# Soft-MoE attention kernel: the first pair's k exchange on ScalarE, the second pair's loads and splits ahead of the bias batches, another order of the attention steps

## The chip, the core and the metric

The kernel runs on one NeuronCore of a Trainium2 chip. Five engines work side by side, each on its own instruction queue, in order: TensorE (PE in the rows; PEld is its weight load), VectorE (DVE), ScalarE (ACT), GpSimd (POOL) and SyncE (SP), which here does nothing but issue DMA transfers. They wait for one another by semaphores. The metric is the device time of one execution in microseconds, as the median of several runs.

## The reference

Attention with a position bias made by a small network, then a soft mixture of experts, then a routed mixture of experts. Cut to what matters here:

```python
# q, k, v: (4, 8, 576, 64)
scores = scale * np.matmul(q, k.transpose(0, 1, 3, 2))
psi_rel = np.log1p(np.abs(rel)); psi_i = np.log1p(np.maximum(pos, 1.0))
h = np.maximum((psi_rel / psi_i)[..., None] @ w1 + b1, 0.0)   # hidden 32
bias = h @ w2                                                 # (576, 576, 8)
attn = softmax(scores + bias.transpose(2, 0, 1)[None])
x = (attn @ v).transpose(0, 2, 1, 3).reshape(2304, 512)
# soft MoE: logits = x @ phi; slots; 8 experts; combine; then a routed MoE
```

## The kernel before

**Stages.** The program has four stages. First come constants. Then **36 bias batches** (`bias_batch`, lines 193 to 215) compute the bias of all heads once and write it to a DRAM tile, `scratch`. Then **16 attention pairs** (a pair is two heads of one of four batches, `ops_of`, line 310) run in a software pipeline. Last come the two expert stages, for which 33 MB of weights are loaded; most of these loads are held until the last transpose DMA of attention (`issue_after(last_dma[0].ins)`, line 818).

**A bias batch** makes four tiles `hid` of 128x576 (line 204 on DVE for three of them, and in 27 of the 36 batches line 206 on ACT for the fourth), multiplies each with two matmuls (line 208) into one of two PSUM buffers `sc`, evicts that on ACT into `ev` (line 211) and writes `ev` to `scratch` by a DMA on SP (line 213). `hid` has 12 buffers, `ev` has six.

**A pair's inputs.** `LK` and `LQ` (lines 333 and 338) load k and q into `tk` and `tq`, one buffer each. On POOL, `KHI`, `KLO`, `QHI`, `QLO` (lines 374 and 376, called the splits below) split them into a high and a low part, `sk` and `sq`, one buffer each. PE transposes those (lines 407 and 432), ACT evicts them (lines 414, 437, 438) into `k0` and the `qT` tiles. `SW` (line 421, on POOL) writes `k1`, which is `k0` with its two halves of 64 partitions exchanged. So the next pair's `LK` waits until `KLO` has read `tk`, the next pair's `LQ` until `QLO` has read `tq`, and the next pair's `KHI` until PE has transposed all of `sk`.

**A pair's work.** For nine tiles: score matmuls from `k0` and `k1` (`QK..p`, line 449), bias added and row minimum on DVE (`QK..e`, line 466), exponential on ACT (`EX..`, line 473). Three double tiles are split into two f16 halves (`HI` on POOL, line 484; `LO` on DVE, line 488), transposed by a DMA (`TD`, line 493, tile `eT`) and multiplied with v (`AV`, lines 574 and 578). The rest goes through PE transposes and line 586. Line 395 splits v on POOL.

**What sets the order.** Each step has a place in the table `SCHED` (or `LAST`, for the last four pairs), in units of a planner's clock, with `II = 14100` units from one pair to the next. All steps are sorted by pair times `II` plus place. Those placed before the first score matmul are emitted ahead of the bias batches (lines 784 to 789), the others behind them, in a region in which every engine keeps exactly the emitted order (`manual_schedule`, line 806). Outside such a region the framework's scheduler orders each queue by its own estimate and may pull the first steps of the region forward among the bias batches.

Of the kernel before, what the change touches and what calls it, by code (L numbers as in the profile page):

```python
# [35 lines left out]
SCHED = {"LK": 5369, "LQ": 0, "LV": 10563, "BA": 23667, "BM": 30989, "TD0": 37335, "TD1": 43011, "TD2": 36576,  # L36
         "KHI": 6999, "KLO": 10045, "QHI": 5298, "QLO": 11325, "VA": 19235, "VH": 21228, "VLO": 27550, "KG0p": 11467,
# [11 lines left out]
LAST = {"LK": [-3065, 3082, 4354, 5430], "LQ": [-995, -2408, -2168, -2345], "LV": [10067, 14234, 12275, 20450],  # L49
         "BA": [18431, 35072, 34832, 22492], "TD0": [39915, 48050, 36190, 24610], "TD1": [49170, 48930, 36590, 25210],  # L50
         "TD2": [37091, 35430, 35150, 24410], "KHI": [3849, 7705, 6112, 5590], "KLO": [7665, 7785, 8536, 5670],
         "QHI": [7168, 4291, 6072, 6590], "QLO": [11035, 10644, 11635, 7150], "VA": [19244, 19466, 20650, 21450],
# [53 lines left out]
def soft_moe_attention_kernel(ctx, tc, q, k, v, w1, b1, w2, phi, mw1, mw2,  # L106
# [203 lines left out]
    def ops_of(n):  # L310
# [106 lines left out]
        @part  # L417
        def SW():
            k0, k1 = kk()
            for i in range(2):  # L420
                pool.tensor_scalar(out=k1[64 * i:64 * i + 64], in0=k0[64 - 64 * i:128 - 64 * i],  # L421
                                   scalar1=1.0, scalar2=1.0, op0=ALU.mult, op1=ALU.mult)
# [363 lines left out]
    for t_, n, x in todo:  # L786
        if t_ < first:
            OPS[n][x]()
# [583 lines left out]
```

## Time and profile before

| what | value |
|---|---|
| median of three runs | 495.49 us (495.05 to 497.6) |
| profiled execution: its time | 498.0 us |
| profiled execution: its span, first to last instruction | 496.2 us |
| mean granted TensorE clock | 0.952 |
| busy in the span: PE, DVE, ACT, POOL | 84%, 70%, 60%, 53% |

By time in the span: constants up to 7.1 us; bias batches to 77.2 us, with the first score result on DVE at 78.7 us; attention to about 350 us; the expert stages to the end. How to read the rows below: a busy row is one instruction or several merged; an idle time names what ended it; a wait names the waiting engine and line, an arrow, and what it waited for.

### The profile page before, as it was taken

To read this page: it belongs to the slowest core of one execution; us is meant where nothing else is said; L and a number is where in the kernel's file an instruction comes from. 1 tells how busy PE (TensorE), PEld (TensorE's weight loads), DVE (VectorE), ACT (ScalarE), POOL (GpSimd) and SP (SyncE) were. 2 spreads that over 40 slices of the span, in tenths; PEclk is the share of its full clock that TensorE was granted. 3 is DMA by queue.
4 is the path that set the end of the run, shared out by engine and by line. 5 is a ranking of instruction groups with operands and counts; after the bars stand their busy time and mean duration, and the time that the engine had idled before them with its cause. 6 is when DMAs were issued, how large, how long until landed. Compare 5 with 4: busy or idle time off the path is not lost.

```text
span 496.2 us, 11535 instructions
## 1 busy us (share of the span) xinstructions
PE 414.4 (84%) x4291; PEld 301.4 (61%) x4291; DVE 346.7 (70%) x824; ACT 298.5 (60%) x631; POOL 262.9 (53%) x245
## 2 busy tenths in 40 slices
PE   4870799797998999889899899897788787779993
PEld 2430356697987899769788799785345311255462
DVE  6990596888887899878889888897547400047564
ACT  3970796788887889779779799783322100027510
POOL 4496001999898799798978788861300000000000
PEclk9995799899999999999999999999899799959998
DMA  6713975799999999999998999799999999572066
GB/s 164 250 49 82 360 274 194 162 193 223 223 215 220 211 212 228 178 228 208 225 215 205 221 178 207 159 205 189 399 387 408 387 387 387 202 264 77 26 198 188
DMA packets 154076, 111.49 MB, mean 225 GB/s; under 512 B 120256, under 2 KB 126912, under 8 KB 154016
## 3 DMA queue, kind: packets, MB, share of 16 engines
q1 hardware_dynamic: 152112, 107.47, 85.8%
q10 hardware_dynamic: 1824, 2.97, 1.8%
q8 instruction: 36, 0.59, 0.5%
q0 software_dynamic: 80, 0.26, 0.2%
q14 instruction: 24, 0.20, 0.1%
HBM read 66.97 MB, written 15.34 MB: 166 GB/s over the span
## 4 chain that ended last, share of the span: by engine, by line
PE 41%; DMA 28%; DVE 10%; issue 8%; ACT 6%; POOL 4%; SPq 1%; ACTq 0%; DVEq 0%; POOLq 0%
DMA eT<-ehl 17%; PE sc L449 9%; DMA x<-in_moe_w_dram 4%; PE av L578 4%; PE sc L208 4%; POOL k L421 3%; PE av L586 3%; PE pt L407 3%; DVE e L466 3%; DMA bias<-in_moe_w_dram 2%; ACT ev L211 2%; PE ph L892 2%; DMA tn<-in_v_dram 2%; PE av L574 2%; DMA w1e<-in_moe_w_dram 1%
## 5 line engine op out<-in xcount | busy, mean ns | idle before, releaser
L466 DVE CUSTOM_DVE_ANT_0 e<-sc,bias 128x576 f32<-128x576 f32 x128 | 93.9, 749 | 25.0 <-PE sc L449 18.8
L449 PE MATMUL sc<-k,qT 128*128 128x288 f32 x512 | 98.6, 318 | 8.6 <-DVE st L466 5.5
L473 ACT ACTIVATE e<-e,st 128x576 f32<-128x576 f32 x128 | 97.3, 779 | 3.5 <-DVE st L466 3.0
L484 POOL TENSOR_SCALAR ehl<-e 128x1152 f16<-128x1152 f32 x48 | 66.1, 1383 | 53.1 <-ACT e L473 49.9
L488 DVE SCALAR_TENSOR_TENSOR ehl<-e,ehl 128x1152 f16<-128x1152 f32 x48 | 81.5, 1699 | 2.1 <-POOL ehl L484 2.1
L449 PEld LDWEIGHTS sc<-k,qT 128*128 128x128 f32 x512 | 73.1, 191 | 15.1 <-DVE st L466 8.4
L421 POOL TENSOR_SCALAR k<-k 64x1152 fp32r<-64x1152 f32 x32 | 75.0, 2343 | 12.6 <-ACT k L437 11.1
L208 PE MATMUL sc<-hid,w2b 128*32 128x288 f32 x576 | 50.0, 440 | 22.4 <-ACT ev L211 19.3
L204 DVE TENSOR_SCALAR hid<-ll,nib 128x576 f32<-128x576 f32 x117 | 53.6, 537 | 16.4 <-PE sc L208 16.4
L208 PEld LDWEIGHTS sc<-hid,w2b 128*32 128x32 f32 x576 | 24.2, 115 | 46.0 <-ACT ev L211 31.9
L578 PE MATMUL av<-v,eT 128*128 128x65 f16 x1152 | 50.2, 193 | 0.0
L578 PEld LDWEIGHTS <-eT 128*128 128x128 f16 x1152 | 42.8, 97 | 1.3 <-issue 0.8
L211 ACT ACTIVATE ev<-sc,offs,ipi 128x576 f32<-128x576 f32 x36 | 30.0, 834 | 21.8 <-DMA scratch<-ev 16.9
L1099 POOL TENSOR_SCALAR Lt<-rk 128x128 f16<-128x128 f32 x1 | 0.3, 298 | 74.3 <-PE pbig L973 74.3
L574 PE MATMUL av<-v,eT 128*128 128x130 f16 x144 | 16.3, 221 | 15.9 <-DMA eT<-ehl 15.9
L586 PE MATMUL av<-eq,tv 128*64 128x192 f32 x320 | 29.5, 331 | 0.0
L979 DVE COPY part<-pbig 128x256 f32<-128x256 f32 x1 | 0.4, 425 | 38.6 <-ACT part L978 38.6
L414 ACT ACTIVATE qT<-pt 128x512 fp32r<-128x512 f32 x32 | 19.1, 602 | 9.8 <-PE pt L407 9.5
L586 PEld LDWEIGHTS av<-eq,tv 128*64 128x64 f32 x320 | 21.6, 137 | 4.9 <-issue 2.4
L574 PEld LDWEIGHTS <-eT 128*128 128x128 f16 x144 | 9.8, 98 | 23.9 <-DMA eT<-ehl 22.1
L978 ACT COPY part<-pbig 128x256 f32<-128x256 f32 x1 | 0.4, 372 | 39.6 <-PE pbig L973 39.6
L395 POOL TENSOR_TENSOR v<-tv,v 128x650 f16<-128x650 f32 x16 | 24.0, 1502 | 0.0
(334 smaller groups left out, 887.2 us busy)
## 6 DMA issues: line engine op xcount, KB each, us to landing
x<-in_moe_w_dram SPq DMA_DIRECT2D x30, 512.0 KB, 10.7
scratch<-ev SPq DMA_DIRECT2D x36, 288.0 KB, 4.5
bias<-scratch SPq DMA_DIRECT2D x16, 576.0 KB, 4.8
tn<-in_v_dram SPq DMA_DIRECT2D x32, 224.0 KB, 4.3
bias<-in_moe_w_dram SPq DMA_DIRECT2D x13, 512.0 KB, 10.2
k<-in_moe_w_dram SPq DMA_DIRECT2D x12, 512.0 KB, 10.2
tq<-in_q_dram SPq DMA_DIRECT2D x16, 288.0 KB, 5.8
tk<-in_k_dram SPq DMA_DIRECT2D x16, 288.0 KB, 4.0
```

Of the source, the lines that this page charges most:

```text
L204: vec.tensor_scalar(out=hid, in0=src, scalar1=nib[:, gi:gi + 1], scalar2=None, op0=ALU.max)
L208: pe.matmul(pb[c * 32:(c + 1) * 32, hh, 0:288], lhsT=w2b, rhs=hid[:, hh * 288:(hh + 1) * 288], start=True, stop=True)
L211: act.activation(ev, pb[:, :, 0:288].rearrange("p a (l u) -> p u a l", u=NU), AF.Identity, bias=offs[not on_act], scale=ipi[:, bt:bt + 1])
L421: pool.tensor_scalar(out=k1[64 * i:64 * i + 64], in0=k0[64 - 64 * i:128 - 64 * i], scalar1=1.0, scalar2=1.0, op0=ALU.mult, op1=ALU.mult)
L449: pe.matmul(sc[:, hh, 0:288], lhsT=l_, rhs=kf[i][:, o:o + 288], start=(i == 0), stop=(i == 1))
L466: vec.tensor_tensor_reduce(out=z["e", t][:, o].rearrange("p (a j) -> p a j", a=2), in0=z.pop(("sc", t, j))[:, :, 0:288], in1=bias_t[hp, t] ...
L473: act.activation(ee, ee, AF.Exp, bias=z["m", t][:, j:j + 1], scale=-1.0, **kw)
L484: pool.tensor_scalar(out=eh[:, 0], in0=z["e", t], scalar1=ES, scalar2=1.0, op0=ALU.mult, op1=ALU.mult)
L488: vec.scalar_tensor_tensor(out=eh[:, 1], in0=z.pop(("e", t)), scalar=ES, in1=eh[:, 0], op0=ALU.mult, op1=ALU.subtract)
L574: pe.matmul(av[:, o:o + 2 * VD], lhsT=eT[:, ei, 4], rhs=v16[:, vi, 4].rearrange("p j d -> p (j d)"), start=firstt and k_ == 0, stop=False)
L578: pe.matmul(av[:, oj:oj + VD], lhsT=eT[:, ei, 5 * j + c], rhs=v16[:, vi, c, j], start=False, stop=lastt and k_ == 2 and c == 3)
L586: pe.matmul(z["av", 1][j * 64:(j + 1) * 64, o], lhsT=tv[:, c, j, 0:64], rhs=z["eq"][:, 4 * j + c if c < 4 else 8], start=False, stop=last ...
```

## The change

- **`SW` of the first pair** runs on ACT as two copies instead of two POOL instructions. The other 15 pairs keep POOL.
- **Early steps.** Beside the steps that are placed early, `LK`, `LQ`, `KHI`, `KLO`, `QHI`, `QLO` of the second pair are emitted ahead of the bias batches.
- **Bias batches** keep their emitted order on SP (`manual_schedule` for SP alone).
- **`SCHED` and `LAST`** are other tables. `II` stays 14100. The pipeline is shorter by the planner's units: its last step, `LG1e`, stands at 68360 instead of 75850.

```diff
-SCHED = {"LK": 5369, "LQ": 0, "LV": 10563, "BA": 23667, "BM": 30989, "TD0": 37335, "TD1": 43011, "TD2": 36576,
+SCHED = {"LK": 0, "LQ": 172, "LV": 9234, "BA": 18742, "BM": 28658, "TD0": 29881, "TD1": 36646, "TD2": 28531,
...
-         "EX11": 33957, "QK20p": 19732, "QK20e": 20133, "EX20": 24208, "QK21p": 20517, "QK21e": 21124, "EX21": 24356,
+         "EX11": 23319, "QK20p": 14985, "QK20e": 15074, "EX20": 20772, "QK21p": 17994, "QK21e": 19507, "EX21": 20879,
...
-         "LO1": 39852, "AV10": 47267, "AV11": 48212, "HI2": 28668, "LO2": 29348, "AV20": 38264, "AV21": 43739,
+         "LO1": 34176, "AV10": 40878, "AV11": 41991, "HI2": 21790, "LO2": 25589, "AV20": 33382, "AV21": 35572,
...
             for i in range(2):
+                if n == 0:
+                    act.copy(k1[64 * i:64 * i + 64], k0[64 - 64 * i:128 - 64 * i])
+                    continue
                 pool.tensor_scalar(out=k1[64 * i:64 * i + 64], in0=k0[64 - 64 * i:128 - 64 * i],
                                    scalar1=1.0, scalar2=1.0, op0=ALU.mult, op1=ALU.mult)
...
+    def x_early(x):
+        return x in ("LK", "LQ", "KHI", "KLO", "QHI", "QLO")
+
     todo = sorted((n * II + place(n, x), n, x) for n in range(NP) for x in OPS[n])
     first = min(SC[x] for x in SC if x[:2] == "QK")
-    for t_, n, x in todo:
-        if t_ < first:
-            OPS[n][x]()
-    todo = [y for y in todo if y[0] >= first]
+    early = [y for y in todo if y[0] < first or y[1] == 1 and x_early(y[2])]
+    for t_, n, x in early:
+        OPS[n][x]()
+    todo = [y for y in todo if y not in early]
...
-    for i, bt in enumerate(order):
-        bias_batch(bt)
-        if bt % 8 == 7 or bt == 35:
-            load_bias(0, bt // 8)
+    with tc.manual_schedule(engines={mybir.EngineType.SP}):
+        for bt in order:
+            bias_batch(bt)
+            if bt % 8 == 7 or bt == 35:
+                load_bias(0, bt // 8)
```

The lines of the changed kernel stand 3 higher than before from line 421 on. Three places show what the change does to the queues.

**SP, among the first bias batches, before** (`tq`, `tk` are the q and k loads: the first row is the second pair's q, the next `tk` its k, the last `tq` and `tk` the third pair's; `tn` and `tl` load the second pair's v; `scratch` rows are the bias writes):

```order
L338 DMA tq<-in_q_dram 128x576
L213 DMA scratch<-ev 128x576
L333 DMA tk<-in_k_dram 128x576
L347 DMA tn<-in_v_dram 64x2x448
L213 DMA scratch<-ev 128x576
L347 DMA tn<-in_v_dram 64x2x448
L350 DMA tl<-in_v_dram 128x1x64
L213 DMA scratch<-ev 128x576 x7
L338 DMA tq<-in_q_dram 128x576
L269 DMA bias_390<-scratch 128x1152
L213 DMA scratch<-ev 128x576
L333 DMA tk<-in_k_dram 128x576
```

and the same place after the change:

```order
L333 DMA tk<-in_k_dram 128x576
L347 DMA tn<-in_v_dram 64x2x448 x2
L213 DMA scratch<-ev 128x576
L338 DMA tq<-in_q_dram 128x576
L350 DMA tl<-in_v_dram 128x1x64
L213 DMA scratch<-ev 128x576 x3
L333 DMA tk<-in_k_dram 128x576
L213 DMA scratch<-ev 128x576
L338 DMA tq<-in_q_dram 128x576
L213 DMA scratch<-ev 128x576 x3
L269 DMA bias_403<-scratch 128x1152
```

The third pair's loads moved forward: its k load stands behind four bias writes and its q load behind five, where its q load stood behind nine and its k load behind ten.

**POOL, from its first split on, before** (`sq`, `sk` are the splits; `k_199` is the first pair's exchange, `k_1046` the second's; `v` is line 395, `ehl` line 484):

```order
L374 TENSOR_SCALAR sq<-tq 128x9x64
L376 TENSOR_TENSOR sq<-tq,sq 128x9x64
L374 TENSOR_SCALAR sk<-tk 128x9x64
L376 TENSOR_TENSOR sk<-tk,sk 128x9x64
L421 TENSOR_SCALAR k_199<-k_198 64x1152 x2
L374 TENSOR_SCALAR sq<-tq 128x9x64
L374 TENSOR_SCALAR sk<-tk 128x9x64
L376 TENSOR_TENSOR sk<-tk,sk 128x9x64
L376 TENSOR_TENSOR sq<-tq,sq 128x9x64
L395 TENSOR_TENSOR v_1014<-tv_166,v_1014 128x650
L484 TENSOR_SCALAR ehl<-e 128x1152 x2
L421 TENSOR_SCALAR k_1046<-k_1045 64x1152 x2
```

and after:

```order
L374 TENSOR_SCALAR sk<-tk 128x9x64
L376 TENSOR_TENSOR sk<-tk,sk 128x9x64
L374 TENSOR_SCALAR sq<-tq 128x9x64
L376 TENSOR_TENSOR sq<-tq,sq 128x9x64
L374 TENSOR_SCALAR sk<-tk 128x9x64
L376 TENSOR_TENSOR sk<-tk,sk 128x9x64
L374 TENSOR_SCALAR sq<-tq 128x9x64
L376 TENSOR_TENSOR sq<-tq,sq 128x9x64
L395 TENSOR_TENSOR v_1022<-tv_166,v_1022 128x650
L487 TENSOR_SCALAR ehl<-e 128x1152 x2
L424 TENSOR_SCALAR k_1071<-k_1070 64x1152 x2
```

The first pair's exchange is gone from POOL's queue, k is split ahead of q, and the second pair's four splits follow the first pair's directly.

**ACT, in the bias batches, before** (`hid` and `ev` are the bias batches'; the first two rows evict the last transposes of the first pair, `qT` its q):

```order
L437 COPY k_198<-pt 128x2x64
L438 ACTIVATE qm_164<-pt 128x2x64
L414 ACTIVATE qT_219<-pt 128x512
L211 ACTIVATE ev<-sc,offs_133,ipi 128x576
L206 ACTIVATE hid<-ll,pib 128x576
L211 ACTIVATE ev<-sc,offs_133,ipi 128x576
L206 ACTIVATE hid<-ll,pib 128x576
L414 ACTIVATE qT_226<-pt 128x512
```

and after:

```order
L440 COPY k_198<-pt 128x2x64
L441 ACTIVATE qm_164<-pt 128x2x64
L414 ACTIVATE qT_217<-pt 128x512
L211 ACTIVATE ev<-sc,offs_133,ipi 128x576
L422 COPY k_199<-k_198 64x1152 x2
L211 ACTIVATE ev<-sc,offs_133,ipi 128x576
L206 ACTIVATE hid<-ll,pib 128x576
L414 ACTIVATE qT_226<-pt 128x512
```

The exchange, two copies of 64x1152, now stands between the evictions of two bias batches; the f16 copy of the first pair's v (line 391), which stood behind the first eviction before, moved behind the first exponential of attention.

## Rows read from the trace of the kernel before

**Rows 1.** Page, part 2: busy tenths in 40 slices of 12.4 us

```profile
PE   4870799797998999889899899897788787779993
...
DVE  6990596888887899878889888897547400047564
```

**Rows 2.** Waits, 0 to 80 us: total, times, longest in us

```profile
PE sc L208 <- ACT ev L211: 19.3, 10, 16.8
ACT ev L211 <- DMA scratch<-ev: 16.9, 1, 16.9
DVE hid L204 <- PE sc L208: 16.4, 2, 15.9
```

**Rows 3.** Timeline of SP's queue: start us, us, engine, line, operation

```profile
16.83 9.79 SPq L213 DMA_DIRECT2D scratch<-ev  x7
44.73 0.33 SPq L338 DMA_DIRECT2D tq<-in_q_dram  x1
```

**Rows 4.** Waits of SP's queue, 0 to 100 us

```profile
SPq L338 <- POOL sq L376: 20.4, 2, 18.0
```

**Rows 5.** Timeline of POOL, 0 to 50 us

```profile
8.80 0.67 POOL L374 TENSOR_SCALAR sq<-tq 128x576 fp32r<-128x576 f32 x1 [5.69 <-DMA tq<-in_q_dram]
...
11.97 1.48 POOL L376 TENSOR_TENSOR sk<-tk,sk 128x576 fp32r<-128x576 f32 x1
20.41 20.07 POOL L421 TENSOR_SCALAR k<-k 64x1152 fp32r<-64x1152 f32 x2 [6.95 <-ACT k L437]
40.56 0.67 POOL L374 TENSOR_SCALAR sq<-tq 128x576 fp32r<-128x576 f32 x1
...
43.30 1.40 POOL L376 TENSOR_TENSOR sq<-tq,sq 128x576 fp32r<-128x576 f32 x1
```

**Rows 6.** Timeline of DVE in the bias batches, from three windows

```profile
7.13 7.50 DVE L204 TENSOR_SCALAR hid<-ll,nib 128x576 f32<-128x576 f32 x10
...
20.14 18.12 DVE L204 TENSOR_SCALAR hid<-ll,nib 128x576 f32<-128x576 f32 x42
...
54.16 1.38 DVE L204 TENSOR_SCALAR hid<-ll,nib 128x576 f32<-128x576 f32 x3 [15.89 <-PE sc L208]
56.08 21.13 DVE L204 TENSOR_SCALAR hid<-ll,nib 128x576 f32<-128x576 f32 x49 [0.54 <-PE sc L208]
78.74 0.76 DVE L466 CUSTOM_DVE_ANT_0 e<-sc,bias 128x576 f32<-128x576 f32 x1 [1.53 <-PE sc L449]
```

**Rows 7.** Line 421 over the whole span: duration ns min/median/max

```profile
L421 POOL TENSOR_SCALAR k<-k x32: 1145/2154/18866, 20.4 to 316.2; 64x1152 fp32r<-64x1152 f32 x32
```

**Rows 8.** Timeline of ACT around the stall

```profile
33.46 0.77 ACT L206 ACTIVATE hid<-ll,pib 128x576 f32<-128x576 f32 x1
51.11 0.83 ACT L211 ACTIVATE ev<-sc,offs,ipi 128x576 f32<-128x576 f32 x1 [16.88 <-DMA scratch<-ev]
```

**Rows 9.** Groups on ACT, 0 to 80 us: count, busy us, mean ns, idle before

```profile
L206 ACT ACTIVATE hid<-ll,pib 128x576 f32<-128x576 f32 x27 | 20.7, 774 | 3.2 <-DVE ll L184 3.2
...
L391 ACT CAST v<-tv 128x650 f16<-128x650 f32 x1 | 0.7, 722 | 0.0
...
L438 ACT ACTIVATE qm<-pt 128x128 fp32r<-128x128 f32 x1 | 0.3, 318 | 0.0
```

**Rows 10.** Busy us by stretch: last bias batches, then the sum over 12 pairs

```profile
54.10:77.30 23.20, 22.25 (x286) 11.36 (x278) 22.51 (x52) 21.48 (x30) 0.00 (x0) 0.95 0.81 288
...
sum 196.45, PE 182.17 PEld 163.37 DVE 168.29 ACT 162.26 POOL 174.77; mean PE 15.18 PEld 13.61 DVE 14.02 ACT 13.52 POOL 14.56
```

**Rows 11.** Waits in the pair loop, 118 to 284 us

```profile
PE av L574 <- DMA eT<-ehl: 10.6, 13, 1.4
...
POOL ehl L484 <- ACT e L473: 6.7, 9, 2.2
```

**Rows 12.** Chain that ended last, in order of time: start us, us

```profile
341.61 6.29 DMA eT<-ehl
...
395.91 10.78 DMA x<-in_moe_w_dram
```

More of the change, by code (lines that the diff above doesn't have):

```diff
@@ L35 @@
 II = 14100
-SCHED = {"LK": 5369, "LQ": 0, "LV": 10563, "BA": 23667, "BM": 30989, "TD0": 37335, "TD1": 43011, "TD2": 36576,
-         "KHI": 6999, "KLO": 10045, "QHI": 5298, "QLO": 11325, "VA": 19235, "VH": 21228, "VLO": 27550, "KG0p": 11467,
[11 rows of a table removed]
[L49 to L52, printed above, removed]
[34 rows of a table removed]
-         "XTp": [64310, 51850, 39350, 25890], "XTe": [64870, 51970, 39670, 26010], "XUp": [67710, 51330, 38990, 25490],
[7 rows of a table removed]
+SCHED = {"LK": 0, "LQ": 172, "LV": 9234, "BA": 18742, "BM": 28658, "TD0": 29881, "TD1": 36646, "TD2": 28531,
+         "KHI": 1475, "KLO": 3042, "QHI": 5285, "QLO": 5664, "VA": 13644, "VH": 17188, "VLO": 20958, "KG0p": 6373,
[11 rows of a table added]
+LAST = {"LK": [-10166, -6928, -3988, -1796], "LQ": [-5398, -7388, -8117, -1676], "LV": [2290, 11539, 13064, 15360],
+         "BA": [10081, 27726, 28502, 17722], "TD0": [38302, 42520, 30580, 19080], "TD1": [41824, 42600, 31820, 19400],
+         "TD2": [34283, 38342, 30500, 18680], "KHI": [-1568, -2561, -824, -1236], "KLO": [5184, -1210, 4446, -1076],
+         "QHI": [1166, 2183, -74, -236], "QLO": [3934, 4449, 6283, 12520], "VA": [12179, 14642, 26100, 15600],
[4 rows of a table added]
+         "LASTp": [6898, 6164, 6523, 13120], "LASTe": [7730, 8486, 12224, 13520], "SW": [11579, 12890, 12744, 14480],
[28 rows of a table added]
+         "XTp": [57100, 45000, 33100, 20040], "XTe": [57340, 45160, 33140, 20160],
+         "XUp": [-243577, 45320, 33340, 19840], "XUe": [59660, 45720, 33420, 19920],
[6 rows of a table added]
+         "FSe": 21400}
 ETB = 4
```

97 rows, old and new, of tables (LAST, SCHED) are left out of this document.

## Prediction

> **What bounds the kernel now.** I read the page's picture of the span first. In the fourth slice, 37 to 50 us, PE and DVE both show 0 and then recover [rows 1]: a stall of the whole machine in the bias batches, before attention has begun. Next the waits of the first 80 us: ACT's eviction waits 16.9 us, once, for the landing of a bias write; PE waits 16.8 us for that eviction; DVE waits 15.9 us for PE [rows 2]. That is one chain, and its root is further up. SP's timeline shows seven bias writes up to 26.6 us, then nothing until the third pair's q load at 44.73 [rows 3], and SP's own waits name the reason: line 338 waited 18.0 us for POOL's `QLO` of the second pair [rows 4]. While that load waits, no bias write behind it on SP can be issued; the six `ev` buffers fill; ACT stops after 34.2 us and goes on at 51.11 [rows 8].
>
> Why was POOL late? Its two exchange instructions for the first pair stand ahead of the second pair's splits and took 20.07 us from 20.41 on [rows 5], one of them 18.9 us where 1.145 us is the shortest of the 32 [rows 7]. DVE ran line 204 without a gap from 20.14 to 38.26 [rows 6]: POOL finished 1.0 us after DVE paused. So POOL's exchange was held back by DVE's stream, and DVE paused only because the stall that this caused had reached it. Then the four splits ran in 4.1 us, 40.56 to 44.70 [rows 5], and SP went on.
>
> Behind it the pair loop: 12 pairs took 196.45 us, 16.37 us each, of which PE is busy 15.18, POOL 14.56, DVE 14.02 [rows 10]. PE at 93% is the limit there; its largest wait is 10.6 us in 166 for the transposed `eT` [rows 11]. After the last `eT` transpose at 341.61 us the chain is the weight loads, 10.8 us a piece [rows 12]. They are held until that transpose, so an earlier end of attention moves the rest forward one for one.
>
> **The change part by part.**
>
> *The stall goes.* It is worth what DVE idled, 15.89 + 0.54 us [rows 6]: DVE is the engine that the bias batches need longest. Its pitch undisturbed is 18.12/42 = 0.43 us, and 117 such instructions take 50.3 us, 1.40 us a batch. In the last bias batches DVE is busy 22.5 of 23.2 us, ACT 21.5 [rows 10]. So without the stall DVE sets the end of this stage.
>
> *The second pair's splits move under DVE's stream.* What they cost is read from the first pair's splits, which ran there: POOL's first took 0.67 us and its last 1.48, as good as their durations in the stall, 0.67 and 1.40 [rows 5], and it was DVE that paid: its ten instructions from 7.13 on took 7.50 us [rows 6] where 10 x 0.43 + 0.1 = 4.4 is undisturbed, so 3.1 us. Before, the second pair's splits ran in the stall and cost nothing; now they cost DVE another 3.1 us. DVE would end at 7.13 + 50.3 + 3.1 + 3.1 = 63.6 us instead of 77.2: a gain of 13.6 us.
>
> By the Trainium skill (SBUF — State Buffer, Who interferes with whom), whichever of a GpSimd instruction and a VectorE instruction in a 2-port mode comes first holds the shared port pair for that one instruction, and the other waits until it is done. The rows of the first pair's splits agree with that; the 18.9 us of the exchange do not, since it let some 40 of DVE's instructions pass. By that rule alone each split waits 0.43 us at most and the sum stands; by the exchange's row it is the first rival below.
>
> *The exchange on ACT.* No row shows it. From below: ACT's 128x128 eviction takes 0.318 us, its 128x650 copy 0.722 [rows 9], so 0.00077 us a column and 1.11 us for 1152 columns. From above: two 576-column activations at 0.774 [rows 9], 1.55 us. Two copies: 2.2 to 3.1 us; I take 2.2, since the 650-column copy is the nearest in kind. ACT loses its 0.72 us copy of v from this stage, so it has 1.5 us more work in 36 batches, and idles 1.7 us in the last 18 alone [rows 10]. In total it fits; but it comes in one piece, with two `sc` buffers ahead of it and 12 `hid` buffers between DVE and PE. It costs DVE between nothing (hidden under the splits' 3.1 us, which fall at the same place) and 2.2 us; I take 0.6. A gain below zero is excluded for it: it adds work.
>
> *SP's queue.* The third pair's k load now waits for `KLO`, its q load for `QLO` of the second pair, behind four and five bias writes. The second pair's `KHI` must wait until PE has transposed the first pair's `sk`; that is over by 20.41 us, when the exchange started behind those transposes' evictions [rows 5]. With 4.3 us for four splits, `QLO` ends by 25 us. The ninth bias write left by 26.6 us [rows 3], so the sixth, at 1.4 us each, is due near 22: it is held 3 us at most, and six `ev` buffers cover 8. Cost nothing; if that cover is gone, it is the first rival.
>
> *The new order of the loop.* The same instructions, 12 pairs in the steady table. It can give back at most what PE idles, 16.37 - 15.18 = 1.19 us a pair or 14 us; `eT` waits are 10.6 of it. `TD0` to `AV00` grows from 1460 to 9245 units, which speaks for fewer such waits; `EX21` to `HI2` shrinks from 4312 to 911, which speaks for more waits of POOL. I take 0, with -5 to +5.5 us around it. The drain of the last four pairs has a new table as well; it is in the same margin.
>
> *Sum.* 13.6 - 0.6 + 0 = 13.0 us: the profiled 498.0 becomes 485.0. The median of the runs lies 2.5 us under the profiled execution, so 495.5 - 13.0 = **482.5 us**.
>
> **The rivals.**
>
> *The splits are held back as the exchange was.* For: 18.9 us beside the same DVE stream [rows 7]. Against: the same kind of instruction, on all 128 partitions, got through at once at 8.80 us [rows 5]. Then the third pair's k load blocks SP behind four bias writes, not nine: ACT stops 5 x 1.4 = 7 us earlier, at 27.2; DVE at 31.3; POOL then needs 2.2 us for `KHI` and `KLO`; ACT goes on 6.4 us after SP is free (44.73 to 51.11), at 39.9, and DVE 3.05 us later, at 42.9. DVE idles 11.6 us instead of 16.4: a gain of 4.6 us, **491**.
>
> *The order is better on the chip as well.* `AV00` finds its `eT` ready: 8 of the 10.6 us come back beside the 13. **474.5**.
>
> *Slower: POOL waits for exponentials.* POOL is in order and has 16.37 - 14.56 = 1.81 us a pair to spare; it waits 0.67 us a pair for ACT's exponentials now [rows 11]. `HI2` stands 3.4 units of a thousand closer behind `EX21`. If all of that became waiting, a pair took 14.56 + 0.67 + 3.4 = 18.6 us. It turns the whole into a loss from 16.37 + 13/12 = 17.45 us a pair, a wait of 2.9 us; at 3.25 us, a pair of 17.8, the loop loses 17.3 us: **500**. Against: the planner moved other steps too, and DVE, ACT and PE shift with POOL.
>
> *It doesn't do what it says.* The stall comes back from another wait on SP, as the q load's on POOL did, and the bias stage ends at the old time: **495.5**.
>
> **How the numbers follow.** Forecast 0.55 (477.5 to 488), splits held back 0.15, better order 0.15, slower loop 0.08, no effect 0.07. The range of 472 to 493 takes in the forecast with its bounds, the held-back splits and nearly all of the better order; outside lie 0.15 and the edges. A measurement tells about 0.5%, 2.5 us, from no change: faster than that 0.85, same 0.07, slower 0.08.
>
> **What would show it.** Right: ACT's wait for a bias write and SP's 18.0 us wait for POOL are gone or under 4 us; the second pair's four splits stand between 17 and 25 us with 0.7 to 1.5 us each; the first score result on DVE at 65 to 67 us instead of 78.74; line 204 shows a second group of stretched instructions; the fourth slice is full; the last transpose near 328.5. Wrong: a split of more than 5 us beside line 204 (first rival); a pair in the loop under 15.8 us (better order) or over 17.4 with POOL waiting for line 476 (slower); a stall of the same length elsewhere (no effect).

## The result and the profile after

The changed kernel takes **492.05 us** (median of six runs, 487.66 to 496.36) against 496.58 for the kernel before beside it (six runs). The ratio is **0.9896**, 95% interval 0.9852 to 0.994: faster, clear of 1.00 but by only about 5 us, where 13 were forecast. The time lies inside the predicted range and 9.6 us above the predicted value; 1.1 of these are the base, which was 495.49 in the runs that the forecast stood on. The profiled execution took 491.48 us, its span is 489.6 where it was 496.2. Runs of one kernel spread by 5 to 10 us on these chips and some executions are disturbed as a whole, so I compare stages in the traces, use medians only for the whole, take the ratios from undisturbed executions alone, and do not read the traces of `lv_lg`, `mix` and `after_again`, which are of disturbed ones, stage by stage.

Five marks cut both spans: the first score result on DVE, the first `AVB` matmul of the first pair (line 586, now 589), the same of the twelfth pair (11 pair periods later), the last transpose DMA and the end.

| stage, us | before | after | gain |
|---|---|---|---|
| to the first score result | 78.74 | 67.03 | 11.7 |
| from there to the first `AVB` | 23.7 | 24.0 | -0.3 |
| 11 pair periods | 181.9 | 187.4 | **-5.5** |
| twelfth `AVB` to last transpose | 57.3 | 56.8 | 0.5 |
| last transpose to the end | 154.6 | 154.4 | 0.2 |

So the start did nearly what was forecast in this execution, and the new order of the loop, which I had taken as nothing, gave almost half of it back.

**The start.** The picture of the span, busy tenths in 40 slices, now of 12.2 us, PE and DVE; the two zeros of [rows 1] in the fourth slice are gone:

```profile
PE   4786997988998989889988999998797777799983
...
DVE  6998977976978989878988898996648100047563
```

POOL at the first and the second pair's splits (start, duration, line, tiles, idle time before):

```profile
7.61 0.89 POOL L374 TENSOR_SCALAR sk<-tk 128x576 fp32r<-128x576 f32 x1 [4.48 <-DMA tk<-in_k_dram]
...
11.01 1.48 POOL L376 TENSOR_TENSOR sq<-tq,sq 128x576 fp32r<-128x576 f32 x1
17.33 7.18 POOL L374 TENSOR_SCALAR sk<-tk 128x576 fp32r<-128x576 f32 x1 [4.84 <-PE pt L435]
24.59 1.41 POOL L376 TENSOR_TENSOR sk<-tk,sk 128x576 fp32r<-128x576 f32 x1
25.97 0.88 POOL L374 TENSOR_SCALAR sq<-tq 128x576 fp32r<-128x576 f32 x1
26.93 1.49 POOL L376 TENSOR_TENSOR sq<-tq,sq 128x576 fp32r<-128x576 f32 x1
```

Three of the second pair's four splits cost what the first pair's do. The first, `KHI`, took 7.18 us, more than ten times the 0.67 that such a split takes in [rows 5]: the first rival's mechanism, on a smaller scale. DVE over the same time, and ACT's exchange:

```profile
7.02 16.96 DVE L204 TENSOR_SCALAR hid<-ll,nib 128x576 f32<-128x576 f32 x32
25.35 14.56 DVE L204 TENSOR_SCALAR hid<-ll,nib 128x576 f32<-128x576 f32 x29 [1.37 <-PE sc L208]
41.35 24.14 DVE L204 TENSOR_SCALAR hid<-ll,nib 128x576 f32<-128x576 f32 x56 [1.44 <-PE sc L208]
67.03 0.76 DVE L469 CUSTOM_DVE_ANT_0 e<-sc,bias 128x576 f32<-128x576 f32 x1 [1.54 <-PE sc L452]
```

```profile
20.93 2.32 ACT L422 CAST k<-k 64x1152 fp32r<-64x1152 f32 x2
```

DVE stood from 23.98 to 25.35 us; `KHI` ended at 24.51, inside that pause. The pause has its root in ACT's exchange: PE waited for the eviction behind those two copies, and with PE stopped DVE came to the end of its `hid` buffers.

```profile
24.15 1.20 PE L208 MATMUL sc<-hid,w2b 128*32 128x288 f32 x16 [2.00 <-ACT ev L211]
```

The 117 instructions took 55.66 us, 5.4 more than 117 x 0.43, and DVE idled 2.81 us (15.89 + 0.54 in [rows 6]). On SP the third pair's q load left at 28.45 us, where [rows 3] has 44.73:

```profile
26.02 0.33 SPq L333 DMA_DIRECT2D tk<-in_k_dram  x1
26.45 0.38 SPq L213 DMA_DIRECT2D scratch<-ev  x1
28.45 0.33 SPq L338 DMA_DIRECT2D tq<-in_q_dram  x1
```

The held `KHI` kept SP waiting as well. Where line 338 waited 18.0 us for POOL [rows 4], the third pair's k load now waits 6.9 us for `KLO` (SP's waits from 0 to 100 us):

```profile
SPq L333 <- POOL sk L376: 9.5, 2, 6.9
```

Of ACT's 16.9 us wait for a bias write [rows 2], this row of the waits from 0 to 80 us (total, times, longest) is left:

```profile
ACT ev L211 <- DMA scratch<-ev: 3.3, 2, 2.9
```

The 2.9 us end at 39.27 us, and DVE's second pause, 1.44 us, stands behind them.

**The loop.** Busy times over the 11 periods, before and then after (us, then PE, PEld, DVE, ACT, POOL with their instructions, granted clock, DMA share, GB/s):

```profile
102.40:284.30 181.90, 167.05 (x2029) 150.39 (x2028) 155.76 (x372) 148.86 (x335) 162.70 (x133) 1.00 1.10 214
```

```profile
91.00:278.40 187.40, 169.73 (x2029) 154.31 (x2028) 160.10 (x369) 149.66 (x334) 162.08 (x132) 0.97 1.03 210
```

The number of matmuls is the same. PE's idle time grew from 14.9 to 17.7 us, its busy time by 2.7, and the clock fell from 1.00 to 0.97. Waits over that stretch, before and then after:

```profile
PE av L574 <- DMA eT<-ehl: 11.9, 14, 1.4
...
POOL sk L374 <- DMA tk<-in_k_dram: 5.7, 4, 2.3
```

```profile
ACT tv L384 <- DMA tn<-in_v_dram: 15.3, 9, 2.9
POOL sk L374 <- DMA tk<-in_k_dram: 10.0, 8, 2.0
...
PE av L577 <- DMA eT<-ehl: 5.0, 4, 1.4
```

The wait for `eT` halved, as the longer distance from `TD0` to `AV00` said. In its place ACT waits for v (lines 384 and 387 scale the loaded v, `tn`, into `tv`), of which the kernel before shows no row in this stretch, and POOL's wait for k grew from 5.7 to 10.0 us. The clock's share is in three places. Windows of after around the first of them: a stretch in which PE had next to nothing to do, until ACT evicted `xT` (a wait of 1.86 us), then three at work:

```profile
114.80:116.70 1.90, 0.05 (x1) 0.03 (x1) 0.98 (x3) 1.86 (x7) 1.42 (x2) 1.00 0.80 178
116.70:118.00 1.30, 1.29 (x10) 1.30 (x11) 0.10 (x1) 0.98 (x3) 1.30 (x2) 0.91 1.20 251
118.00:121.00 3.00, 3.00 (x15) 2.97 (x14) 1.57 (x5) 2.28 (x5) 2.51 (x3) 0.50 1.09 206
121.00:123.00 2.00, 2.00 (x30) 1.99 (x28) 2.00 (x3) 1.56 (x5) 1.43 (x1) 0.95 0.51 207
```

A granted clock of 0.50 is the lower level, 1.2 GHz; it stayed for some 3.4 us. The same came near 149 and near 217 us, with PE waits of 2.08 and 2.23 us (line 642, the transposes of the output tile `ot`, which wait for a PSUM buffer that DVE's evictions of the logits free). The three periods that hold these stretches took 18.2, 18.6 and 18.8 us; the other eight average 16.48. In the loop of before the longest PE wait is 1.37 us and the clock stays at 1.00.

### The profile page after: what moved, and what is told of

Same layout as the page of the kernel before. It is cut to its first block, busy times and chain, and to the rows that moved or that the text cites. A ratio compares the mean times of both kernels' runs of the same rounds, so it can differ in the third digit from the quotient of the medians.

```text
span 489.6 us, 11571 instructions
## 1 busy us (share of the span) xinstructions
PE 420.0 (86%) x4291; PEld 302.8 (62%) x4291; DVE 354.4 (72%) x824; ACT 301.7 (62%) x633; POOL 252.6 (52%) x243
## 4 chain that ended last, share of the span: by engine, by line
PE 33%; DMA 33%; DVE 16%; ACT 8%; issue 5%; POOL 3%; SPq 1%; ACTq 0%; DVEq 0%; POOLq 0%
DMA eT<-ehl 9%; PE sc L452 7%; DVE ehl L491 7%; DMA x<-in_moe_w_dram 7%; DMA bias<-in_moe_w_dram 4%; DMA scratch<-ev 4%; DVE e L469 3%; ACT ev L211 3%; PE av L589 3%; PE av L581 2%; PE sc L208 2%; PE ph L899 2%; DMA tn<-in_v_dram 2%; DMA k<-in_moe_w_dram 2%; DMA bias<-scratch 2%
## 5 line engine op out<-in xcount | busy, mean ns | idle before, releaser
L491 DVE SCALAR_TENSOR_TENSOR ehl<-e,ehl 128x1152 f16<-128x1152 f32 x48 | 83.8, 1746 | 0.5 <-POOL ehl L487 0.4
L487 POOL TENSOR_SCALAR ehl<-e 128x1152 f16<-128x1152 f32 x48 | 60.2, 1262 | 7.9 <-ACT e L476 4.5
L204 DVE TENSOR_SCALAR hid<-ll,nib 128x576 f32<-128x576 f32 x117 | 55.7, 557 | 2.8 <-PE sc L208 2.8
L395 POOL TENSOR_TENSOR v<-tv,v 128x650 f16<-128x650 f32 x16 | 31.0, 1936 | 44.6 <-ACT v L391 44.6
L424 POOL TENSOR_SCALAR k<-k 64x1152 fp32r<-64x1152 f32 x30 | 51.5, 1717 | 4.6 <-ACT k L414 1.4
L581 PEld LDWEIGHTS <-eT 128*128 128x128 f16 x1152 | 43.8, 99 | 0.9
L374 POOL TENSOR_SCALAR sk<-tk 128x576 fp32r<-128x576 f32 x16 | 18.1, 1131 | 21.8 <-DMA tk<-in_k_dram 14.5
L376 POOL TENSOR_TENSOR sq<-tq,sq 128x576 fp32r<-128x576 f32 x16 | 27.0, 1690 | 1.1
L544 PE MATMUL pt<-ident,e 128*128 128x128 f32 x144 | 24.8, 285 | 0.5 <-ACT eq L549 0.5
L980 PE MATMUL pbig<-x,hT 128*32 128x512 f32 x76 | 20.5, 623 | 4.8 <-DMA x<-in_moe_w_dram 4.8
```

The source lines that it names most:

```text
L204: vec.tensor_scalar(out=hid, in0=src, scalar1=nib[:, gi:gi + 1], scalar2=None, op0=ALU.max)
L395: pool.tensor_tensor(out=z["v16"][:, 1], in0=tv, in1=z["v16"][:, 0], op=ALU.subtract)
L487: pool.tensor_scalar(out=eh[:, 0], in0=z["e", t], scalar1=ES, scalar2=1.0, op0=ALU.mult, op1=ALU.mult)
L491: vec.scalar_tensor_tensor(out=eh[:, 1], in0=z.pop(("e", t)), scalar=ES, in1=eh[:, 0], op0=ALU.mult, op1=ALU.subtract)
L581: pe.matmul(av[:, oj:oj + VD], lhsT=eT[:, ei, 5 * j + c], rhs=v16[:, vi, c, j], start=False, stop=lastt and k_ == 2 and c == 3)
```

## The experiments

Two theories of the loop's loss stood against each other: the PE waits at line 642 and the low clock behind them (theory 1), and ACT waiting for v (theory 2). Of the start it was open whether `KHI` was held up by DVE's stream or by its place, and what that cost. "Loop" below is 11 periods; "first" the first score result on DVE. Ratios are to the kernel before, on the same chip.

**old_order and old_start: the two halves of the change.** The three edits of the start with the old tables, and the new tables without those edits:

```diff
 # old_order: the changed kernel with
-SCHED, LAST = the new tables
+SCHED, LAST = the tables of before
 # old_start: the kernel before with
-SCHED, LAST = the tables of before
+SCHED, LAST = the new tables
```

> The three edits of the start (exchange on ScalarE, early splits, bias writes in order on SP) with the tables of before. Both theories of the loop (the waits for a PSUM buffer behind VectorE's low halves; ScalarE's waits for v) put the loss into the new tables: the first score result stays near 67 us, 11 pairs take 182 us again instead of 187.4, and the time is about 484.5. If the loop were slower because of its earlier start and not of its tables, 11 pairs take 187 us and the time is 490.

> The new tables with the start of before (exchange on GpSimd, no early splits). The exchange is held back by VectorE's stream again and SP's queue with it: the first score result at 75 to 79 us, the loop as in the changed kernel (187 us for 11 pairs), 500 to 503 in all. If the new tables were no slower than the old ones, 496.

| | time | ratio | first | loop |
|---|---|---|---|---|
| before | | 1 | 78.74 | 181.9 |
| after | 492.05 | 0.9896 (0.9852 to 0.994) | 67.03 | 187.4 |
| old_order | 490.74 | 0.9853 (0.9785 to 0.9921) | 72.20 | 180.7 |
| old_start | 500.42 | 1.0005 (0.9969 to 1.004) | 74.13 | 186.4 |

The loop's loss goes with the tables: 186.4 with the new ones, 180.7 with the old, whatever the start. With the old tables the start came 5.2 us later than in after, though it had all three edits: DVE idled 6.1 us in it instead of 2.81. So the start and the time of old_order are misses (67 and 484.5 us were expected), and the new tables have a share in the earlier start: alone they bring the first score result 4.6 us forward, the three edits alone 6.5, both 11.7.

**lg_first: theory 1.** The logits' evictions on DVE, for which line 642 waits, moved ahead of `LO2`:

```diff
-"LG0e": 54444, ... "LG1e": 68360
+"LG0e": 53250, ... "LG1e": 67300
```

> The changed kernel with the evictions of the logits (LG0e, LG1e) ahead of the low half LO2 in VectorE's order, in the steady table. Theory 1 (TensorE waits some 2 us in every other pair for the PSUM buffer that these evictions free, and then runs at the lower clock for about 3 us): the waits of line 642 on line 694 or 696 go, the clock stays at 1.00 in the loop, 11 pairs take about 183 us, 487 in all. Theory 2 (ScalarE's waits for the v loads set the pace): no change, 491 to 492.

495.71 us, ratio 0.9914 (0.9875 to 0.9954). Its loop:

```profile
92.40:279.60 187.20, 167.63 (x2031) 149.54 (x2030) 160.13 (x369) 149.45 (x334) 163.50 (x132) 1.00 1.02 210
```

The clock is back at 1.00 and PE is busy 2.1 us less, but the loop takes 187.2 us as before: PE idles 19.6 us instead of 17.7, in waits for other evictions. So the low clock was a price, but taking away its cause did not set the pace free. Theory 1 falls as the whole cause.

**lv_early, lvk_early, va_late: theory 2.** On SP the v loads (`LV`) stand behind the transposing read `TD1`, which holds SP for 2.7 to 4.3 us. lv_early puts them ahead of it, lvk_early the k load too; va_late leaves SP alone and moves ACT's scaling of v back.

```diff
 # lv_early
-"LV": 9234
+"LV": 8400
 # lvk_early
-"LK": 0, "LV": 9234
+"LK": -5660, "LV": 8400
 # va_late, from the second pair on
-"VA": 13644
+"VA": 16500
```

> The changed kernel with the v loads ahead of the transpose TD1 on SP's queue in the steady table. Theory 2 (ScalarE waits 13 us in ten pairs for these loads, and what stands behind it is late): those waits go, 11 pairs take about 184 us, 488. Theory 1 (the PSUM buffer): ScalarE's waits go but 11 pairs stay at 186 to 188 us, and the time at 491 to 492; since TD1 is issued 2 us later, a wait for eT may come back.

> The changed kernel with ScalarE's copy of v placed 2.9 thousand units later in its pair (from the second pair on); the queue of SP stays as it is, so the v load still stands behind the transposing read. If the loop's loss is ScalarE standing at the copy for a load that has not landed, those waits (13.4 us in eight copies) go, and 11 pairs take about 183 us instead of 187.4, the run about 488. If the loads themselves, or the order of SP as such, set the pace, the waits on ScalarE go but 11 pairs stay above 186. First score result stays at 67 to 69 us under both.

> The changed kernel with the v load and the k load of a pair both ahead of the transposing read on SP. Moving the v load alone brought 11 pairs from 187.4 to 182.9 us and left GpSimd waiting 8.6 us for k. If loads behind the transposing read are what paces the loop, GpSimd's waits for k go too and 11 pairs take 181 to 182.5 us, the kernel before's 181.9. If only ScalarE's wait counted, they stay at 183 plus or minus 0.6. If the earlier loads come to wait for their buffers and hold the transposing read behind them, more than 184.

SP in one pair, before, after and then lv_early:

```profile
153.84 6.35 SPq L493 DMA_TRANSPOSE eT<-ehl  x2
160.25 0.57 SPq L269 DMA_DIRECT2D bias<-scratch  x1
160.91 1.31 SPq L347 DMA_DIRECT2D tn<-in_v_dram  x2
```

```profile
123.88 2.71 SPq L496 DMA_TRANSPOSE eT<-ehl  x1
126.67 1.31 SPq L347 DMA_DIRECT2D tn<-in_v_dram  x2
128.07 0.56 SPq L350 DMA_DIRECT2D tl<-in_v_dram  x1
```

```profile
138.41 1.32 SPq L347 DMA_DIRECT2D tn<-in_v_dram  x2
139.84 0.56 SPq L350 DMA_DIRECT2D tl<-in_v_dram  x1
140.50 4.09 SPq L496 DMA_TRANSPOSE eT<-ehl  x1
```

The kernel before has the v load behind transposing reads too, even two of them. What its table has and the new one lacks is distance: from `LV` to `VA`, ACT's scaling of v, it leaves 8672 units, the new one 4410, va_late 7266.

The loops of lv_early, va_late and lvk_early:

```profile
92.80:275.70 182.90, 167.37 (x2031) 152.26 (x2030) 158.36 (x369) 148.73 (x334) 162.04 (x132) 0.98 1.07 214
```

```profile
94.80:281.30 186.50, 170.90 (x2031) 153.24 (x2032) 158.99 (x371) 150.55 (x334) 158.02 (x132) 0.98 1.05 211
```

```profile
93.70:281.70 188.00, 171.19 (x2029) 156.62 (x2028) 158.56 (x369) 148.70 (x334) 164.16 (x132) 0.95 1.04 208
```

lv_early: 490.7 us, ratio 0.9842 (0.9808 to 0.9876), and 4.5 of the 5.5 us are back. ACT's wait for v is gone and PE's wait for `eT` is back:

```profile
PE av L577 <- DMA eT<-ehl: 8.6, 8, 2.6
```

va_late: 495.44, ratio 0.9943 (0.9911 to 0.9975); ACT's wait for v is gone here too, but the loop takes 186.5, so ACT's wait in itself is not the loss. Moving ACT's step only made other waits: PE waits 5.9 us in ten waits for ACT's evictions of `eq`, of which after shows 0.5. lvk_early: 497.81, ratio 0.9993 (0.996 to 1.0027), a miss: POOL's wait for k fell to 2.7 us, and the loop is the longest of the three.

The periods show where that time went. They are parted here into those that hold a stretch at 1.2 GHz and the rest:

| | with a stretch at 1.2 GHz | mean of the other periods |
|---|---|---|
| before | none | 16.54 |
| after | 18.2, 18.6, 18.8 | 16.48 |
| lg_first | none | 17.02 |
| lv_early | 19.2, 20.0 | 15.97 |
| lvk_early | 18.4, 19.9, 18.7, 21.5 | 15.64 |
| va_late | 19.4, 18.4 | 16.52 |

Not all of a long period is the clock's doing: the seventh of before took 19.6 us and the eighth and tenth of lg_first 18.5 and 18.4, all at a granted clock of 1.00. The three periods of after that hold the low stretches are longer than the same ones of lg_first by 1.5, 1.0 and 0.3 us only.

Earlier loads make a quiet period shorter than the kernel before has it (16.22 us without its longest), 15.97 and then 15.64 us. But the transposing read goes behind them, PE now stands up to 2.6 us at a time for `eT` or at line 642, and the clock dropped twice in lv_early and four times in lvk_early, for some 3.4 us each and once for nearly 7. Against lv_early, PE in lvk_early is busy 3.8 us longer with as many matmuls and idles 1.3 us more: there the low clock takes back most of what the loads gave.

**lv_lg.** Both edits together (`LV` 8400, `LG0e` 53250, `LG1e` 67300).

> The changed kernel with both edits to the loop: the v load ahead of the transposing read (which took ScalarE's waits away and left 3.4 us of TensorE's time lost to the lower clock), and the logits' evictions ahead of LO2 (which kept the clock up, and left ScalarE waiting for v). If the two losses are separate, 11 pairs take 179.5 to 181 us, under the kernel before's 181.9, and the run 486 to 488. If removing one wait only uncovers another, 11 pairs stay at 182.5 to 185 and the run at 489 to 493.

495.87 us, ratio 0.9972 (0.9923 to 1.002), where lv_early has 0.9842. A miss: the two gains do not add. Which wait came up stays open.

**pool_swap, hid8, keep: what held `KHI` up.** The exchange back on POOL with the early splits kept; eight `hid` buffers between DVE and PE in place of twelve; and the first pair's `QHI` issued five times, with the same values, so that POOL does not idle long.

```diff
 # pool_swap
-                if n == 0:
-                    act.copy(k1[64 * i:64 * i + 64], k0[64 - 64 * i:128 - 64 * i])
-                    continue
 # hid8
-tc.tile_pool(name="hid", bufs=12, side="right")
+tc.tile_pool(name="hid", bufs=8, side="right")
 # keep
+                for _ in range(5 if n == 0 and x == "q" else 1):
                     pool.tensor_scalar(out=sx[:, :, 0, :], in0=t, ...)
```

> The changed kernel with the first pair's exchange back on GpSimd, the early splits kept. If a GpSimd instruction is held off until VectorE's stream of L204 pauses, and it is ScalarE's lump of two copies that makes it pause at 24 us, then without the lump the exchange or the second pair's KHI behind it takes over 10 us and the first score result comes at 72 to 75 us instead of 67.0. If each GpSimd instruction only shares with VectorE instruction by instruction, no one takes over 4 us, and the first score result comes at 66 to 68 us.

> The changed kernel with eight instead of twelve buffers between L204 and TensorE, so that VectorE can run less far ahead and must stop sooner and more often. If GpSimd is let in only when VectorE's stream pauses, the second pair's first split (7.18 us) comes in earlier and takes under 4 us, and the third pair's loads are issued 2 to 4 us sooner; the first score result comes at 66 to 68.5 us, depending on what VectorE loses by stopping. If the length of that split has another cause, it stays at 6 to 8 us.

> The changed kernel with the first pair's QHI issued five times in place of once, the same values each time, so that GpSimd is idle for 1 to 2 us instead of 4.8 us before the second pair's KHI. In the runs so far KHI took over 7 us wherever GpSimd had been idle for 3.55 us or more beside a running L204, and 0.73 us after 3.12 us of idling. If the length of VectorE's run without GpSimd in it decides, KHI takes under 1.1 us now and QLO of the second pair ends by 23 us instead of 28.4. If it is chance or the place in the program, KHI takes about 7 us again. The first score result comes at 66.5 to 69 us, since the four added instructions slow VectorE.

One execution each: 493.21, 496.54 and 492.5 us, and the first score result at 66.95, 66.63 and 67.19. POOL in pool_swap, then hid8, then keep:

```profile
17.26 0.73 POOL L374 TENSOR_SCALAR sk<-tk 128x576 fp32r<-128x576 f32 x1 [3.12 <-PE pt L432]
18.08 1.49 POOL L376 TENSOR_TENSOR sk<-tk,sk 128x576 fp32r<-128x576 f32 x1
19.66 2.56 POOL L421 TENSOR_SCALAR k<-k 64x1152 fp32r<-64x1152 f32 x2
```

```profile
16.84 2.02 POOL L374 TENSOR_SCALAR sk<-tk 128x576 fp32r<-128x576 f32 x1 [3.98 <-PE pt L435]
```

```profile
18.98 0.74 POOL L375 TENSOR_SCALAR sk<-tk 128x576 fp32r<-128x576 f32 x1 [3.12 <-PE pt L436]
19.80 1.49 POOL L377 TENSOR_TENSOR sk<-tk,sk 128x576 fp32r<-128x576 f32 x1
23.39 0.90 POOL L375 TENSOR_SCALAR sq<-tq 128x576 fp32r<-128x576 f32 x1 [2.10 <-PE pt L408]
```

pool_swap refuted my reading that only ACT's copies let POOL in: with the exchange on POOL nothing was held up, the exchange took 2.56 us instead of 20.07, and DVE ran its 117 instructions in one piece, 58.38 us. So **the stall goes without the move of the exchange to ACT**, at least where `KHI` gets in at once. It got in here after 3.12 us of idling, because the first k had landed later, and what the move is worth where `KHI` is held was not run. In after it was ACT's two copies that brought the pause in which `KHI` ended; old_start, with the exchange on POOL and without the other two edits of the start as well, had `KHI` held twice as long, until the old stall, 9.2 us of idling on DVE:

```profile
17.12 14.05 POOL L374 TENSOR_SCALAR sk<-tk 128x576 fp32r<-128x576 f32 x1 [3.98 <-PE pt L432]
```

Nor was the fixed order on SP undone alone, so the early splits and that order are not parted. hid8 shows what ends a hold: with eight buffers DVE runs full sooner, pauses at 18.34 us, and `KHI` is through after 2.02 us instead of 7.18. keep shows what starts one: with 3.12 us of idling in place of 4.84, `KHI` took 0.74 us. Its first score result came no later for the four added instructions, though `QLO` ended at 25.9 us where 23 were expected.

**mix, mix_keep, mix2, mix2_keep, lv_keep, after_again: joining the good start with a good loop.** mix has the new tables for what is emitted ahead of the bias batches and the old tables behind; mix2 also takes the third pair's loads and the place of the first `VH` from the new order, so that every engine's order is that of after up to the first score. "keep" is `QHI` five times in mix_keep, six in the other two.

```diff
 # mix: after the early steps are emitted
+    todo = sorted((n * II + place_l(n, x), n, x) for n in range(NP) for x in OPS[n] if (n, x) not in done)
 # mix2: place_l is the place in the old tables, but for
+        if n == 0 and x == "VH":
+            return 23000
+        if n == 2 and x in ("LK", "LQ"):
+            return place(n, x)
```

> The start of the changed kernel, its table for what is emitted ahead of the bias batches included, and the tables of the kernel before for all the rest. If the new table's gain is all in the start and its loss all in the loop, the first score result comes at 66.5 to 68.5 us and 11 pairs take 180.5 to 182: last transpose near 329.5, run 484.5 to 487, faster than both kernels. If the start's gain hangs on the order behind it (the third pair's loads on SP, the copy of v), the first score result comes at 70 us or later, the run at 488 to 491.

> As mix, with the first pair's QHI issued five times so that GpSimd never idles long beside L204. If a held-up KHI costs mix anything, this one starts 0.5 to 4 us earlier; if VectorE sets the end of the bias batches anyway, the added instructions make it 0 to 1.5 us later. 11 pairs 180.5 to 182 either way.

> Up to the first score product the changed kernel's order on every engine, the third pair's loads and the first copy of v included; behind it the tables of the kernel before. If start and loop are separate: first score result at 66.5 to 68 us, 11 pairs in 180.5 to 182.5, last transpose near 329.5, run 484 to 487, and 1 to 1.5% faster than the changed kernel beside it. If the old loop pays for an earlier start with a longer fill, 11 pairs take over 184 and the run equals the changed kernel's.

> The changed kernel itself, beside mix2 on one chip: first score result 67, 11 pairs 186 to 188, run 0.985 to 0.994 of the kernel before.

> As mix2, with the first pair's QHI issued six times. If the held-up KHI is what lets the bias writes come late, KHI takes under 1.1 us, ScalarE's wait for bias writes in the first 68 us falls from 5.4 to under 1.5, and the first score result comes at 66.6 to 68 us instead of 70.3; with 11 pairs at 180.5 to 183 the run is 486 to 489. If the late writes have another cause, it comes at 69.5 to 71 and the run stays at 490 to 492.

> The changed kernel with the v load ahead of the transposing read and the first pair's QHI issued six times. First score result at 66.6 to 68 us instead of lv_early's 69.1 if the held-up KHI costs that, 69 to 70 if not; 11 pairs 182 to 184, the run 487 to 490 or 490 to 492.

| | time | ratio | first | loop |
|---|---|---|---|---|
| mix | 488.3 | 0.9855 (0.9726 to 0.9983) | | |
| mix_keep | 494.47 | 0.9961 (0.9898 to 1.0024) | 73.28 | 180.1 |
| mix2 | 491.55 | 0.9834 (0.978 to 0.9889) | 70.30 | 183.1 |
| after_again, beside mix2 | 496.83 | 0.9916 (0.9878 to 0.9953) | | |
| mix2_keep | 490.1 | none | 71.29 | 180.0 |
| lv_keep | 494.49 | none | 71.13 | 184.4 |

For the last two no ratio is given; the kernel before beside them ran from 487.1 to 502.3, median 498.64. The loop of mix2_keep:

```profile
96.60:276.60 180.00, 166.63 (x2030) 150.40 (x2029) 155.70 (x371) 148.65 (x335) 162.24 (x133) 1.00 1.08 216
```

The loop is settled: behind the new start the old tables take 180.0 to 183.1 us, while the new ones take 186.4 to 191.0, behind either start, where the loads on SP are left alone (after, old_start, lg_first, va_late, pool_swap, hid8, keep). In mix2 one PE wait of 2.28 us brought the clock down once, and that period took 18.3 us against 16.3 in mix2_keep. The start is not settled: mix2 has the instructions of after up to the first score and came 3.3 us later, with `KHI` held 7.18 us in both. The kernels whose edits concern only the loop (lg_first, lv_early, va_late, lvk_early) came at 68.71 to 69.61, so the 67.03 of after lies at the early end, and differences of 2 to 3 us between single starts settle nothing. In mix2 ACT's wait for bias writes was longer:

```profile
ACT ev L270 <- DMA scratch<-ev: 5.4, 3, 3.9
```

That wait is 3.3 us in after, 5.4 in mix2, and 0.9 in keep, and DVE's pause behind it 1.44, 3.81 and 0. So a held `KHI` may cost 0 to 3 us through late bias writes; why they are later in mix2 than in after is not shown. I expected the repeated `QHI` to win that back in mix_keep, mix2_keep and lv_keep, and it did not (in mix2_keep the wait is still 3.1 us): POOL in mix2_keep, with DVE below it:

```profile
19.54 0.74 POOL L434 TENSOR_SCALAR sk<-tk 128x576 fp32r<-128x576 f32 x1 [2.69 <-PE pt L495]
20.36 1.50 POOL L436 TENSOR_TENSOR sk<-tk,sk 128x576 fp32r<-128x576 f32 x1
25.25 4.34 POOL L434 TENSOR_SCALAR sq<-tq 128x576 fp32r<-128x576 f32 x1 [3.39 <-PE pt L467]
```

```profile
29.43 4.26 DVE L263 TENSOR_SCALAR hid<-ll,nib 128x576 f32<-128x576 f32 x7 [0.37 <-PE sc L267]
```

`KHI` got in at once, but `QHI` now came 3.39 us after the step ahead of it, and was held until DVE's pause of 0.37 us at 29.06.

mix2 is the best placed against after: beside it on one chip its ratio is 0.9834 against 0.9916, some 4 us, and five of its six executions lie under the lowest of after's twelve, 492.36, though the ends of the two intervals overlap. lv_early and mix2_keep have medians of 490.7 and 490.1 in other comparisons.

## Why the prediction was right and wrong

**The stall goes: right.** DVE idles 2.81 us instead of 16.43, the fourth slice is no longer empty, ACT's wait for a bias write is 2.9 us at the longest, where under 4 was forecast. SP's longest wait for POOL shrank from 18.0 to 6.9 us, which is not under 4.

**The second pair's splits: one of four wrong.** The sum had DVE at 64.2 us with everything in it and the first score result between 65 and 67; DVE ended at 65.49, the result came at 67.03. The stretch under the splits and ACT's exchange was priced at 6.8 us and measured 5.4, since `KHI` took no turns with DVE but stood outside. Beside it came 2.81 us of DVE idling: 1.37 us behind ACT's exchange, for which the sum had 0.6, and 1.44 behind a late bias write, for which it had nothing. With them the 6.8 became 8.2. The first rival named the mechanism and the sign to look for, "a split of more than 5 us" beside line 204; but it expected a hold until the old stall (a gain of 4.6 us; its own numbers, 16.4 less 11.6, make 4.8), and the hold ended after 7.18 us, when ACT's exchange had stopped PE and then DVE. What I had used against it, that the first pair's splits got through, did not bear on it: those came to POOL when line 204 had run for less than 2.5 us.

**The exchange on ACT: right in size, its worth open.** 2.32 us for two copies, 2.2 forecast; DVE paused 1.37 us for it, 0.6 forecast. In pool_swap's one execution the start is as early without it, which I had not asked; there `KHI` was not held.

**SP's queue: half right.** I had it held 3 us at most and six `ev` buffers to cover 8. Behind the held `KHI` it stood 6.9 us, ACT then waited 2.9 us for a write, and DVE paused 1.44 us, 3.81 in mix2. Where POOL was let in (keep, pool_swap) it cost nothing, but DVE's instructions took nearly as much longer: first score result at 67.2 and 66.95.

**The new order: the step that failed.** The sum's term for the new order of the loop was 0, with a bound of +5.5; over 11 pairs it measured +5.5, and that is nearly half of what the start gained. I had read the two distances in the tables that were easy to read, `TD0` to `AV00` and `EX21` to `HI2`. The first did what it said, the `eT` wait halved. The second did nothing: POOL's wait for exponentials fell from 6.7 to 2.5 us, and the rival built on it, 500, did not come. What I did not look at was the v load, which stands behind `TD1` in the new table, with half the old distance to ACT's use of it: moving it ahead of `TD1` returned 4.5 us. Moving ACT's use back instead (va_late) returned 0.9, so the wait on ACT is not the whole mechanism. Nor did I ask whether fewer, longer PE waits cost more than many short ones; here three waits of about 2 us came with three stretches at 1.2 GHz. How the loss divides between loads and clock stays open, since lg_first, va_late and lvk_early each took away one wait and met another.

**The better-order rival** has something in it: quiet periods of 15.64 to 15.97 us in lvk_early and lv_early are shorter than any of the old order's means. In lvk_early the clock takes it back.

**The chances.** 0.85 for faster was borne out; 0.55 for 477.5 to 488 was too much for a sum whose loop term was a guess. The -5 to +5.5 around it just held the loop's +5.5, and it should have widened the forecast and not only the range.

## What to carry to other kernels

When a table of places is replaced, compare the order on every queue, SP's too, and look at what each load now stands behind; price the loop from that, not from the two distances that look largest. Judge an order by its longest TensorE waits as well as by their sum, since waits of about 2 us were often followed here by 3.4 us at half the clock. And undo each part of a change alone: one of the parts here could be undone without a loss in the one execution that was run, and another cost half of what the rest gave.

## What the runs showed of the hardware

**A GpSimd instruction beside an unbroken stream of VectorE.** The cases of a split or exchange on POOL that came to a running line 204 after POOL had idled for over 1 us, ordered by that idle time. The first split of each kernel is left out: line 204 had run for less than 2.5 us when it came, and it got in at once each time.

| idle before, us | where | took, us |
|---|---|---|
| 1.83 | mix_keep, `KHI` | 0.73 |
| 2.10 | keep, `QHI` | 0.90 |
| 2.69 | mix2_keep, lv_keep, `KHI` | 0.74 |
| 3.12 | keep, pool_swap, `KHI` | 0.74, 0.73 |
| 3.38 to 3.39 | mix_keep, mix2_keep, lv_keep, `QHI` | 4.33, 4.34, 4.34 |
| 3.55 | lv_early, `KHI` | 7.18 |
| 3.98 | hid8, lvk_early, old_start, `KHI` | 2.02, 7.19, 14.05 |
| 4.8 to 5.0 | after, old_order, lg_first, va_late, mix2, `KHI` | 7.0 to 7.2 |
| 6.95 | before, exchange [rows 5] | 18.87 |

Up to 3.12 us it is let in at once and then takes turns with VectorE; from 3.38 on it stands until VectorE pauses, and a pause of 0.37 us is enough. The border is read from these cases alone; only keep and its kin set the idle time by an edit. The point within VectorE's instruction at which GpSimd's came does not sort them: at 0.30 us `KHI` was let in (keep) and held (lv_early), at 0.14 us `QHI` was let in (keep) and held (mix2_keep). By the Trainium skill (SBUF — State Buffer, Who interferes with whom) whoever issues first holds the shared ports for that one instruction. The upper half of the table agrees with it; the lower half does not, since some 15 of VectorE's instructions went by in 7.18 us. Why the time since GpSimd's last instruction matters is not shown.

**TensorE's clock inside a busy loop.** In the loop of after waits of 1.86 to 2.23 us came with 3.4 us each at a granted clock of 0.50, the lower level. In lg_first, mix2_keep and before, whose longest PE waits in that stretch are 1.73, 1.65 and 1.37 us, it stayed at 1.00. The length of the wait does not decide alone: in lv_early waits of 2.58 and 2.22 us, both for `eT`, were not followed by a drop, and waits of 2.28 and 2.04 us at line 642 were; in hid8 waits of 2.28 and 2.27 us at line 642 were not, and one of 1.71 us was; in lvk_early one drop came behind waits of 0.66 and 1.27 us. What decides beside the length is not shown.
